# Attention and MLP kernel: the second head's query projection cut into tiles, placed beside the first head's steps, into a bank of the PV accumulators

## The chip, the cores and the metric

One core of a Trainium2 chip. The metric is the device time of one execution in microseconds (us), as a median of several. The kernel before takes 1239.27 us (3 runs, 1239.21 to 1239.27).

## The reference, cut to what matters

```python
xn = layernorm(x)                                   # x: 2048 x 512
q = (xn @ wq).reshape(1, 2048, 32, 128)             # 32 heads of 128
p = softmax(einsum("bhqd,bhkd->bhqk", q, k_cache) * 128 ** -0.5)
o = einsum("bhqk,bhkd->bhqd", p, v_cache)           # 2048 keys
s = o.reshape(1, 2048, 4096) @ wo
h = relu(xn @ w1 + b1) ** 2                         # 1792 hidden
return x + s * silu(h @ w2 + b2)
```

All inputs are bfloat16. The queries are worked off in four blocks of 512, and in each block the 32 heads one after the other: 128 "heads" g in all, of eight steps each.

## The kernel before: what the change touches

TensorE runs, per step, a scores group (`gen_scores`), a group of products with V (`gen_pv`), and between them up to three matmuls of fill-in work (`fill_one`): query projections of later heads, MLP, output products. ScalarE (ACT) does the exponentials; VectorE (DVE) the casts out of PSUM. PSUM has eight banks: four for scores (psA), two for PV (psO), two for fill-in work (psF).

The opening differs. For head 0 the layernorm is not ready, so its four query tiles of 128 are normalised, transposed and projected one by one, and a step handles one query tile against half of the keys. So PV of steps 0 to 3 (query tiles 0 and 1) writes psO bank 0, and only steps 4 to 7 write bank 1.

```python
def first_proj(i):                     # head 0, query tile i: four matmuls of 128 columns
    for c in range(NDC):
        t_proj[0] = E(PE, partial(_mm, out=bankF(0)[:, i * P:(i + 1) * P],
                                  lhsT=wq_sb[:, 0, c, :], rhs=xnT[:, c, i * P:(i + 1) * P], ...),
                      deps=[t_wqfill[0], tok_xT[0][i], t_q0[i - 1] if i else None], ...)

def first_evac(i):                     # its cast to bfloat16, which the scores wait for
    t_evac[0] = t_q0[i] = E(DV, partial(_copy, out=qt_sb[:, 0, i * P:(i + 1) * P], ...))

def job_proj(g):                       # heads 1 to 127: four matmuls of 512 columns, one per fill_one
    def mm(n, bank):
        t = E(PE, partial(_mm, out=bankF(bank), lhsT=wq_sb[:, i, n, :], rhs=xnT[:, n, js], ...), ...)
    def evac(bank, step):
        t_evac[g] = E(DV, partial(_copy, out=qt_sb[:, g % NQS, :], in_=bankF(bank)), ...)

# order of the loads on the SyncE queue          # the opening, from the first scores on
load_v0(0)                                       gen_scores(0); gen_scores(1)
load_v0(1)                                       first_proj(1); first_evac(1)
fill_wq(1)                                       gen_pv(0); gen_scores(2); first_transpose(2)
fill_k(1)                                        gen_scores(3); first_proj(2); first_evac(2)
                                                 gen_pv(1); gen_scores(4); first_transpose(3)
                                                 gen_scores(5); gen_pv(2); first_proj(3); first_evac(3)
                                                 fill_one(0); fill_one(0)     # half of job_proj(1)
                                                 gen_pv(3); gen_scores(6); gen_scores(7)
                                                 fill_one(0); fill_one(0)     # the other half
                                                 gen_pv(4); gen_pv(5)         # then the main loop
```

The softmax here doesn't subtract the row's maximum and nothing guards it: scores larger than these inputs give would overflow.

## Time and profile before

| | before |
|---|---|
| time, median | 1239.27 us |
| span in the profile | 1237.5 us |
| TensorE's share of the chain that ended last | 98% |
| first scores start | 7.63 us |
| head 3's projection starts | 21.97 us |
| between the two ("the stage") | 14.34 us |

Everything that the change moves on TensorE lies between the first scores and the first matmul of head 3's projection. VectorE's timeline of the kernel before (start, duration, what it did, idle time ahead of it) shows the casts that TensorE waits for:

```profile
14.20 0.29 DVE L179 CAST qt_sb<-psF 128x128 bf16<-128x128 f32 x1 [0.70 <-PE psF L152]
16.41 0.69 DVE L179 CAST qt_sb<-psF 128x512 bf16<-128x512 f32 x1 [1.92 <-PE psF L152]
17.02 0.42 DVE L179 COPY o_un<-psO 128x258 f32<-128x258 f32 x1
...
20.53 0.69 DVE L165 TENSOR_TENSOR o_bf<-o_un,rden 128x512 bf16<-128x512 f32 x1
21.14 0.68 DVE L179 CAST qt_sb<-psF 128x512 bf16<-128x512 f32 x1
21.75 0.16 DVE L179 CAST b1f<-psF 128x14 f32<-128x14 bf16 x1
```

The first is head 0's query tile 3, the second head 1's queries, the fifth head 2's queries; the last three stand one behind the other, and the hole that they make in TensorE's timeline is the last of the opening:

```profile
20.98 0.59 PE L152 MATMUL psA<-qt_sb,kT 128*128 128x512 bf16 x2
21.97 0.38 PE L152 MATMUL psF<-xnT,wq_sb 128*128 128x512 bf16 x1 [0.40 <-DVE b1f L179]
```

Two matmuls of 512 columns end their occupancy at 20.98 + 0.43 = 21.41, so 0.56 us are empty. The view names b1f, which ended last; by the code the matmul waits for its psF bank, which the cast of head 2's queries frees. The packed trace, read one instruction at a time, agrees: the semaphore instruction of TensorE that ends this wait starts at 21.87, 0.04 behind the end of that cast (21.83) and ahead of the end of b1's (21.91).

### The profile page before, as it was taken

To read this page: it belongs to the slowest core of one execution; us is meant where nothing else is said; L and a number is where in the kernel's file an instruction comes from. 1 tells how busy PE (TensorE), PEld (TensorE's weight loads), DVE (VectorE), ACT (ScalarE), POOL (GpSimd) and SP (SyncE) were. 2 spreads that over 40 slices of the span, in tenths; PEclk is the share of its full clock that TensorE was granted. 3 is DMA by queue.
4 is the path that set the end of the run, shared out by engine and by line. 5 is a ranking of instruction groups with operands and counts; after the bars stand their busy time and mean duration, and the time that the engine had idled before them with its cause. 6 is when DMAs were issued, how large, how long until landed. Compare 5 with 4: busy or idle time off the path is not lost.

```text
span 1237.5 us, 26703 instructions
## 1 busy us (share of the span) xinstructions
PE 1221.4 (99%) x11666; PEld 818.6 (66%) x11873; DVE 472.9 (38%) x953; ACT 1053.6 (85%) x1044; POOL 32.0 (3%) x73
## 2 busy tenths in 40 slices
PE   9999999999999999999999999999999999999998
PEld 7666666666666666666666666666666666666666
DVE  4453333244435332334444532233344333324333
ACT  7888888888888888888888888888888888888885
POOL 1010000000002000000000200000000000000000
PEclk9999999999999999999999999999999999999999
DMA  9999988777888787877788888787788788778761
GB/s 209 217 235 180 191 178 140 128 139 140 144 154 166 143 161 133 133 141 146 135 132 169 171 141 142 137 150 137 133 145 149 147 154 157 138 134 146 146 123 31
DMA packets 686868, 185.41 MB, mean 150 GB/s; under 512 B 673536, under 2 KB 685568, under 8 KB 686752
## 3 DMA queue, kind: packets, MB, share of 16 engines
q1 hardware_dynamic: 684656, 179.62, 80.7%
q0 software_dynamic: 1424, 3.81, 1.1%
q8 instruction: 94, 1.54, 0.5%
q10 hardware_dynamic: 672, 0.26, 0.1%
q14 instruction: 22, 0.18, 0.1%
HBM read 96.60 MB, written 2.10 MB: 80 GB/s over the span
## 4 chain that ended last, share of the span: by engine, by line
PE 98%; issue 1%; DVE 1%; DMA 0%; ACT 0%; POOL 0%; DVEq 0%
PE psO L157 38%; PE psA L152 35%; PE psF L152 25%; PE psA L157 0%; DMA x_ln<-in_A_x_dram 0%; DVE out_t L165 0%; PE psF L196 0%; DVE tmp_t L175 0%; ACT pT L161 0%; DVE xnT L179 0%; DVE st_t L200 0%; DVE o_bf L165 0%; DVE qt_sb L179 0%; POOL rstd L165 0%; DVE o_un L179 0%
## 5 line engine op out<-in xcount | busy, mean ns | idle before, releaser
L161 ACT ACTIVATE pT<-psA 128x1024 bf16<-128x1024 f32 x1024 | 1043.6, 1023 | 165.0 <-PE psA L152 119.7
L157 PEld LDWEIGHTS psO<-v_sb,pT 128*128 128x128 bf16 x8192 | 547.9, 98 | 240.8 <-issue 13.1
L157 PE MATMUL psO<-v_sb,pT 128*128 128x129 bf16 x8192 | 631.2, 220 | 0.9 <-ACT pT L161 0.4
L152 PE MATMUL psA<-qt_sb,kT 128*128 128x512 bf16 x1837 | 562.3, 379 | 10.2
L179 DVE COPY o_un<-psO 128x258 f32<-128x258 f32 x256 | 97.4, 422 | 398.5 <-PE psO L157 397.7
L152 PE MATMUL psF<-xnT,wq_sb 128*128 128x512 bf16 (+1 forms) x514 | 167.1, 374 | 0.8 <-DVE b1f L179 0.4
L152 PE MATMUL psF<-wo_all,oT 128*128 128x512 bf16 x479 | 163.4, 379 | 0.1
L152 PEld LDWEIGHTS psA<-qt_sb,kT 128*128 128x128 bf16 x2032 | 156.9, 98 | 0.1
L179 DVE CAST qt_sb<-psF 128x512 bf16<-128x512 f32 (+1 forms) x131 | 88.7, 677 | 103.7 <-PE psF L152 98.0
L152 PEld LDWEIGHTS psF<-xnT,wq_sb 128*128 128x128 bf16 x524 | 50.6, 98 | 60.8 <-issue 1.2
L165 DVE TENSOR_TENSOR o_bf<-o_un,rden 128x512 bf16<-128x512 f32 x128 | 88.5, 692 | 4.7 <-DVE rden L183 0.3
L171 DVE TENSOR_SCALAR r_t<-psF,b1f 128x512 bf16<-128x512 f32 x56 | 42.0, 750 | 116.9 <-PE psF L152 116.9
L152 PEld LDWEIGHTS psF<-wo_all,oT 128*128 128x128 bf16 x480 | 46.9, 98 | 56.4
L152 PE MATMUL psF<-xnT,w_sb 128*128 128x512 bf16 x224 | 77.1, 379 | 0.0
L152 PE MATMUL psF<-w_sb,h2T 128*128 128x512 bf16 x223 | 73.7, 379 | 0.0
L152 PEld LDWEIGHTS psF<-w_sb,h2T 128*128 128x128 bf16 x224 | 21.9, 98 | 26.4
L152 PEld LDWEIGHTS psF<-xnT,w_sb 128*128 128x128 bf16 x224 | 21.9, 98 | 26.4
L165 DVE TENSOR_TENSOR z_t<-psF,b2bc 128x512 f32<-128x512 f32 x16 | 11.1, 692 | 68.3 <-PE psF L152 63.8
L165 DVE TENSOR_TENSOR acc<-psF,acc 128x512 f32<-128x512 f32 x28 | 19.3, 689 | 30.0 <-PE psF L152 30.0
L208 POOL DMA_DIRECT2D out_dram<-out_t x12 | 6.7, 554 | 890.4 <-DVE out_t L165 890.4
L183 DVE RECIPROCAL rden<-o_un 128x4 f32<-128x4 f32 x128 | 22.9, 179 | 4.4
L165 DVE TENSOR_TENSOR h2T<-r_t 128x512 bf16<-128x512 bf16 x56 | 23.8, 425 | 1.9
(44 smaller groups left out, 162.2 us busy)
## 6 DMA issues: line engine op xcount, KB each, us to landing
v_sb<-in_A_v_cache_dram SPq DMA_DIRECT2D x127, 512.0 KB, 4.7
wq_sb<-in_A_wq_dram SPq DMA_DIRECT2D x127, 128.0 KB, 3.4
wo_all<-in_A_wo_dram SPq DMA_DIRECT2D x4, 1024.0 KB, 6.3
w_sb<-in_B_w_dram SPq DMA_DIRECT2D x14, 256.0 KB, 5.1
oT<-o_bf SPq DMA_TRANSPOSE x128, 4.0
x_t<-in_A_x_dram POOLq DMA_DIRECT2D x16, 128.0 KB, 3.2
kT<-in_A_k_cache_dram SPq DMA_TRANSPOSE x127, 4.5
x_ln<-in_A_x_dram SPq DMA_DIRECT2D x15, 128.0 KB, 3.7
```

The costliest lines, as they stand in the source:

```text
L152: return e.matmul(out, lhsT, rhs, start=start, stop=stop)
L157: return e.matmul(out, lhsT, rhs, start=start, stop=stop, skip_group_check=True)
L161: return e.activation(out, in_, func, bias=bias, scale=scale)
L165: return e.tensor_tensor(out, in0, in1, op)
L171: return e.tensor_scalar(out, in0, scalar1=scalar1, scalar2=scalar2, op0=op0, op1=op1)
L179: return e.tensor_copy(out, in_)
L183: return e.reciprocal(out, in_)
L208: return e.dma_start(out, in_)
```

## The change

Head 1's projection leaves its two places near the end of the opening. It is done per query tile, right behind head 0's projection of the same tile (tile 0 together with tile 1), where TensorE is meant to be waiting for ACT or VectorE anyway. The psF banks are taken then, so it writes psO bank 1, which nobody needs between the transposes of the first keys and step 4; one cast empties it. Its weights must come earlier, so their load moves ahead of the two value loads.

```diff
+    def second_proj(i):
+        for c in range(NDC):
+            t_proj[1] = E(PE, partial(_mm, out=bankO(1)[:, i * P:(i + 1) * P],
+                                      lhsT=wq_sb[:, 1, c, :], rhs=xnT[:, c, i * P:(i + 1) * P],
+                                      start=(c == 0), stop=(c == NDC - 1)),
+                          deps=[t_wqfill[1], tok_xT[0][i], t_k0[1]], inc=(c == NDC - 1))
+
+    def second_evac():
+        t_evac[1] = E(DV, partial(_copy, out=qt_sb[:, 1, :], in_=bankO(1)), deps=[t_proj[1]])
 ...                                                      (gen_pv)
                   deps=[t_exp[pi], t_v0[k % 2] if g == 0 else t_vfill[g], t_ones,
+                        t_evac[1] if g == 0 and b == 1 else None,
 ...                                                      (list of fill-in jobs)
-    for g in range(1, NG):
+    for g in range(2, NG):
 ...                                                      (loads)
+    fill_wq(1)
     load_v0(0)
     load_v0(1)
-    fill_wq(1)
 ...                                                      (opening)
     first_evac(1)
+    second_proj(0)
+    second_proj(1)
     gen_pv(0)
 ...
     first_evac(2)
+    second_proj(2)
     gen_pv(1)
 ...
     first_evac(3)
+    second_proj(3)
+    second_evac()
-    fill_one(0)
-    fill_one(0)
     gen_pv(3)
     gen_scores(6)
     gen_scores(7)
-    fill_one(0)
-    fill_one(0)
     gen_pv(4)
```

## The prediction

> **What bounds the kernel now.** I first read the busy shares and the chain that ended last on the page of the kernel before.
>
> ```profile
> PE 1221.4 (99%) x11666; PEld 818.6 (66%) x11873; DVE 472.9 (38%) x953; ACT 1053.6 (85%) x1044; POOL 32.0 (3%) x73
> ...
> PE 98%; issue 1%; DVE 1%; DMA 0%; ACT 0%; POOL 0%; DVEq 0%
> PE psO L157 38%; PE psA L152 35%; PE psF L152 25%; PE psA L157 0%; DMA x_ln<-in_A_x_dram 0%; DVE out_t L165 0%; PE psF L196 0%; DVE tmp_t L175 0%; ACT pT L161 0%; DVE xnT L179 0%; DVE st_t L200 0%; DVE o_bf L165 0%; DVE qt_sb L179 0%; POOL rstd L165 0%; DVE o_un L179 0%
> ```
>
> TensorE (PE) carries 98% of the chain: PV products (psO), scores (psA), and projections, MLP and output products (psF). Busy time alone would not prove it, since matmul ends are modelled, but the chain says the same. So the change can gain in two ways only: fewer array cycles, or fewer holes between matmuls.
>
> Then I listed TensorE's whole-run waits by releaser. After the 1.0 us at the start there are three: 0.4 us for ACT pT, 0.4 us for DVE b1f, 0.2 us for DVE xnT. That view hides short holes, because a matmul counts as busy until its modelled end. So I read the opening in TensorE's timeline (start, duration, count, what it waited for):
>
> ```profile
> 7.63 1.05 PE L157 MATMUL psA<-qt_sb,kT 128*128 128x128 bf16 x16
> 8.52 0.39 PE L152 MATMUL psF<-xnT,wq_sb 128*128 128x128 bf16 x4
> 9.35 0.63 PE L157 MATMUL psO<-v_sb,pT 128*128 128x129 bf16 x8 [0.45 <-ACT pT L161]
> ...
> 11.16 0.40 PE L152 MATMUL psF<-xnT,wq_sb 128*128 128x128 bf16 x4
> 11.40 0.62 PE L157 MATMUL psO<-v_sb,pT 128*128 128x129 bf16 x8
> 12.04 0.61 PE L157 MATMUL psA<-qt_sb,kT 128*128 128x128 bf16 x8
> 12.64 0.40 PE L196 MATMUL psF<-ident,xn_t 128*128 128x128 bf16 x4
> ...
> 13.77 0.82 PE L152 MATMUL psF<-xnT,wq_sb 128*128 128x128 bf16 x5
> 14.43 0.62 PE L157 MATMUL psO<-v_sb,pT 128*128 128x129 bf16 x8
> 14.88 1.06 PE L157 MATMUL psA<-qt_sb,kT 128*128 128x128 bf16 x16
> 15.77 0.59 PE L152 MATMUL psF<-xnT,wq_sb 128*128 128x512 bf16 x2
> 16.21 1.07 PE L157 MATMUL psO<-v_sb,pT 128*128 128x129 bf16 x16
> 17.24 0.59 PE L152 MATMUL psA<-qt_sb,kT 128*128 128x512 bf16 x2
> ```
>
> The reader takes starts from it, not durations. Sixteen scores start at 7.63 and the next group at 8.52, so a 128-column matmul occupies 0.89/16 = 0.056 us; a pair of 512-column ones takes 16.21 - 15.77 = 0.44, or 0.216 each. A hole is the next start less the start plus count times that. Two things to see: a hole of 9.35 - (8.52 + 0.225) = 0.60 us before the first PV group, which waits for the first exponential (ACT, 8.27 to 9.29), and the second head's four 512-column projections sitting where no hole is (two inside the x5 row at 13.77, which lacks one record, and two at 15.77). Smaller holes: 11.85 to 12.04 (0.19, for the cast of the first head's third query tile, DVE 11.60 to 11.89), 12.49 to 12.64 (0.15, for xn_t), and 17.11 to 17.24 (0.13, for the cast of the second head's queries, DVE 16.41 to 17.10). After 22 us the timeline shows a closed row of groups.
>
> **What the Trainium skill says.** "TensorE: Matmul & The Clock Gate", section "Back-to-back issue gap", gives the warm spacing as N/2.4 + 2.5 ns: 56 ns at 128 columns, 216 at 512. The trace agrees (0.056 and 0.216 us). The same section's "sustained" 81 and 131 ns are not what this trace shows, so I use the measured ones. "PSUM — Partial Sum Buffer", section "PSUM bank collisions raise a hardware error", asks for guards by bank, not by address: so PV of query tiles 2 and 3 of head 0, which write the borrowed bank, must wait for the whole cast out of it, which is the wait the change adds. "DMA: Bandwidth & Descriptors", section "Queues, rings and completion order", says that descriptors on each DMA engine's ring are consumed in order. So moving the weight load ahead of the two value loads brings it forward and pushes them back. The trace agrees in tendency: first-half values, second-half values and weights, issued at 3.06, 3.5 and 4.16, landed after 4.9, 5.5 and 5.2 us, that is at 7.96, 9.05 and 9.36.
>
> **The change part by part.**
>
> *Removed:* the second head's projection, 4 x 0.216 = 0.86 us of TensorE, all on the path: 0.43 before PV step 3 and 0.43 before PV step 4.
>
> *Added:* 16 matmuls of 128 columns, 16 x 0.056 = 0.90 us; the array work is thus equal within 0.04 us. Their places decide the gain.
> - Tiles 0 and 1 (8 x 0.056 = 0.45) go after the first head's second projection, at 8.75, into the hole of 0.60. They end at about 9.20, before the PV group is released at 9.35. Cost 0.
> - Tile 2 (0.225) goes before PV step 1: 11.39 to 11.61. That PV ends at 12.06 instead of 11.85, and the scores behind it could not start before 12.04 anyway. Cost about 0.02, and the 0.15 hole for xn_t swallows it. Cost 0.
> - Tile 3 (0.225) goes in after the fourth projection, at 13.995, where there is no hole. Cost 0.225.
>
> *Sum up to PV step 4:* 0.225 - 0.86 = -0.64 us.
>
> *Moved:* the 512-column cast of the second head's queries (0.69 us on DVE) leaves 16.41 for about 14.5, after the cast of tile 3 (14.20 to 14.49). It ends near 15.2. PV step 4, the first user of the borrowed bank, would start at 15.57: the new wait is met with about 0.4 us to spare. The scores of head 1 no longer wait for that cast: another -0.13, the hole at 17.11.
>
> *Do the dependences follow the shift?* Working forward: PV step 3 runs 14.22 to 14.67; the scores of step 6 need the tile-3 cast, which releases at 14.49 + 0.15 = 14.64 (0.15 is the cast-to-start delay seen at 11.89 to 12.04), so they just fit. Their exponential starts 0.65 later, as before (15.53 - 14.88), at 15.32 and ends near 16.34. Scores of steps 6 and 7 and PV steps 4 and 5 end at 14.67 + 0.89 + 0.91 = 16.47, where the first scores of head 1 reuse the buffer freed at 16.34 to 16.40. They fit by under 0.1 us. So those scores start at about 16.47 instead of 17.24: -0.77 us.
>
> *Transfers.* The weights of head 1, now first of three, should land between 7 and 8 (estimate from the landings above: two thirds of a microsecond after the last x tile at 2.55 + 4.2 = 6.7), and are needed at 8.75. First-half values should land near 9.36 - 1.09 = 8.3, since all three still end at 9.36 and the second half takes 9.05 - 7.96 = 1.09; needed at 9.35. Second-half values land near 9.4, needed at about 11.6. None bites. Everything queued behind keeps its place and amount.
>
> *After 22 us* the comparison of the two instruction orders shows no other difference on any engine: the projection came out of slots of the opening, not of the fill-in rhythm of the main loop. Only the parity of the two psF banks flips, and both banks are alike. So the end moves by the same 0.77: 1239.27 - 0.77 = 1238.5 us, or 0.06%.
>
> **The rivals.**
> 1. *The gain is lost to a wait in the opening.* The hole of 0.56 us at 21.41 to 21.97 (the next projection waits for the cast of head 2's queries, DVE 21.14 to 21.82, behind the reciprocal and the normalisation of head 0) stays and could grow if its DVE chain did not move. For: DVE is in order there. Against: that chain begins when PV step 7 ends, which moves with TensorE. If it stood still, about nothing would be gained: 1239.2.
> 2. *The early weights come late and TensorE waits in order.* For: the load's issue took 2.28 us in its old place, so that queue is congested. Against: it goes in ahead of what congested it. If it landed as late as before (9.36), the tiles would run 9.4 to 9.85, PV 0 and what follows would move by 0.5, and the gain would shrink to about 0.3: 1239.0. The same if the first-half values were over 1 us later than before.
> 3. *ACT takes over in the opening.* It idles 0.91 us before the exponential of step 6; TensorE arriving earlier uses that up, and at 16.47 the margin is under 0.1 us. If exponentials bound there, some 0.1 to 0.3 of the 0.77 is lost: 1238.7.
> 4. *More than counted.* If the 0.56 hole closed as well, the gain would be 1.3: 1237.9. I see no part of the change that closes it.
>
> **Range and chances.** Every path but one lies in 1237.9 to 1239.2, and the three runs before lay within 0.06 us. A chip other than that one may differ by some tenths; so 1238.0 to 1239.1 for 8 in 10. Two per cent is 24.8 us, thirty times the gain, and everything the change touches lies in the first 22 us: within 2% has 0.99, the rest is for a surprise.
>
> **What would show it right or wrong.** In the changed kernel's timeline: eight psO<-xnT,wq_sb matmuls at about 8.75 and the first PV still at 9.35 (later would mean weights or values late); scores of step 4 still near 12.05; PV step 3 near 14.2; the cast of the second head from psO ending near 15.2, and no hole of TensorE before PV step 4; the first 512-column scores near 16.5; the hole near 21 still about 0.5 us long and 0.8 earlier. A shift of the opening that does not reappear at the end would make the argument wrong, as it would show that something other than TensorE's order sets the end.

## The result, and the profile after

1238.70 us (6 runs, 1238.42 to 1238.91) against 1239.28 (6 runs, 1239.21 to 1239.48) for the kernel before. The ratio is 0.9995, with a 95% interval of 0.9982 to 1.0008: "same" at 2%. A ratio here is the mean time of one kernel's fast runs over that of the other's of the same rounds, so not quite the ratio of the medians quoted. The interval is wider than the effect, but no run of one kernel overlaps the other's, here or in the repeat below. What rests on tenths of a microsecond below rests on the traces, and the times only agree with it.

TensorE's timeline of the changed kernel:

```profile
7.76 1.05 PE L157 MATMUL psA<-qt_sb,kT 128*128 128x128 bf16 x16 [0.23 <-DVE qt_sb L179]
8.65 0.39 PE L152 MATMUL psF<-xnT,wq_sb 128*128 128x128 bf16 x4
8.87 0.61 PE L152 MATMUL psO<-xnT,wq_sb 128*128 128x128 bf16 x8
9.48 0.63 PE L157 MATMUL psO<-v_sb,pT 128*128 128x129 bf16 x8
...
11.53 0.39 PE L152 MATMUL psO<-xnT,wq_sb 128*128 128x128 bf16 x4
11.76 0.62 PE L157 MATMUL psO<-v_sb,pT 128*128 128x129 bf16 x8
12.21 0.61 PE L157 MATMUL psA<-qt_sb,kT 128*128 128x128 bf16 x8
12.78 0.40 PE L196 MATMUL psF<-ident,xn_t 128*128 128x128 bf16 x4
...
14.13 0.39 PE L152 MATMUL psO<-xnT,wq_sb 128*128 128x128 bf16 x4
14.36 0.62 PE L157 MATMUL psO<-v_sb,pT 128*128 128x129 bf16 x8
14.81 1.06 PE L157 MATMUL psA<-qt_sb,kT 128*128 128x128 bf16 x16
15.70 1.07 PE L157 MATMUL psO<-v_sb,pT 128*128 128x129 bf16 x16
16.61 0.59 PE L152 MATMUL psA<-qt_sb,kT 128*128 128x512 bf16 x2
...
21.34 0.38 PE L152 MATMUL psF<-xnT,wq_sb 128*128 128x512 bf16 x1 [0.40 <-DVE b1f L179]
```

Read it from the first scores. Before, the first PV group came 9.35 - 7.63 = 1.72 us behind them; now 9.48 - 7.76 = 1.72, with eight more matmuls in between. The scores of step 6 (the second x16 row) come at 7.05 instead of 7.25, PV step 4 at 7.94 instead of 8.58, head 1's first scores at 8.85 instead of 9.61. The stage takes 21.34 - 7.76 = 13.58 us instead of 14.34: 0.76 less.

The new cast is where it was meant to be, in VectorE's timeline of the changed kernel:

```profile
14.33 0.29 DVE L179 CAST qt_sb<-psF 128x128 bf16<-128x128 f32 x1 [0.70 <-PE psF L152]
14.56 0.69 DVE L179 CAST qt_sb<-psO 128x512 bf16<-128x512 f32 x1
```

It ends at 15.25, ahead of PV step 4 at 15.70. The shift lasts to the end: head 1's first scores start 17.24 - 16.61 = 0.63 us earlier by the clock of the span, and VectorE's last instruction starts at 1234.61 instead of 1235.24, again 0.63.

The profile shows 0.63 and not 0.76 because in this one profile the first scores came 0.13 later. The matmuls of the opening have two durations. In the profile of the changed kernel those that transpose the first keys (of psO<-ident,kT) are at 314 ns in the median and 219 at the least; in that of the kernel before the median is 219 and the most is 314:

```profile
L196 PE MATMUL psO<-ident,kT x16: 219/314/314, 4.8 to 6.6; 128*128 128x128 bf16 x16
```

```profile
L196 PE MATMUL psO<-ident,kT x16: 219/219/314, 4.8 to 6.4; 128*128 128x128 bf16 x16
```

The two views give the count, the least, the median and the greatest duration. The ends of matmuls are modelled, but the starts in the packed traces say the same: the step from one start to the next falls from 107 to 56 ns 4.5 us after the first matmul in the kernel before, and 5.3 us after it in the changed one. So TensorE was still at its slow pace for longer. The Trainium skill, "TensorE: Matmul & The Clock Gate", section "Part 1: The HAM clock gate (the "warmup" mystery)", says that the clock is released by a free-running window, at a moment that varies by half a microsecond either way. The window may be the cause, but the half microsecond is not what is seen here: over the eleven profiles the step falls anywhere from 2.9 us (x7) to 5.7 us (x6) after the first matmul. Most of that does not reach the first scores, which started from 7.51 to 7.97. The mean granted clock reads 1.00 in all eleven and shows none of it, because the clock records begin only where the step falls (within 0.1 us, in the ten profiles that have records). In two of the eleven (x7 and x8 below) a late landing of the first keys held the first scores up instead. Either way it is chance from run to run, and the repeat of the same changed kernel below shows it.

### The profile page after: what moved, and what is told of

The parts are those of the page before. It is cut to its first block, busy times and chain, and to the rows that moved or that the text cites. A ratio compares the mean times of both kernels' runs of the same rounds, so it can differ in the third digit from the quotient of the medians.

```text
span 1236.8 us, 26934 instructions
## 1 busy us (share of the span) xinstructions
PE 1232.1 (100%) x11885; PEld 819.5 (66%) x11885; DVE 472.5 (38%) x953; ACT 1054.5 (85%) x1044; POOL 32.1 (3%) x73
## 4 chain that ended last, share of the span: by engine, by line
PE 99%; DVE 0%; issue 0%; POOL 0%; DVEq 0%; POOLq 0%
PE psO L157 38%; PE psA L152 36%; PE psF L152 25%; PE psA L157 0%; DVE out_t L165 0%; PE psO L196 0%; DVE tmp_t L175 0%; PE psF L196 0%; DVE qt_sb L179 0%; PE psO L152 0%; DVE o_bf L165 0%; DVE o_un L179 0%; DVE xnT L179 0%; POOL warm L187 0%; DVE rden L183 0%
## 5 line engine op out<-in xcount | busy, mean ns | idle before, releaser
L152 PE MATMUL psA<-qt_sb,kT 128*128 128x512 bf16 x2032 | 604.3, 379 | 0.0
```

Of the source, the lines that this page charges most:

```text
L152: return e.matmul(out, lhsT, rhs, start=start, stop=stop)
```

## The experiments

Nine runs in three series, each timed in five rounds; all are "same" at 2%, so the stage decides, read from one profile of each run, and the times only agree. "Mean difference" is the mean time less that of the kernel before in the same series.

| run | median, us | before, us | mean difference | first scores | stage, us |
|---|---|---|---|---|---|
| before | | 1239.28 | | 7.63 | 14.34 |
| the change | 1238.70 | 1239.28 | -0.62 | 7.76 | 13.58 |
| x0_after_again | 1238.51 | 1239.27 | -0.77 | 7.56 | 13.58 |
| x1_order_only | 1239.25 | 1239.27 | +0.09 | 7.57 | 14.35 |
| x2_old_order | 1239.21 | 1239.27 | -0.03 | 7.67 | 14.22 |
| x3_miss_hole | 1238.97 | 1239.27 | -0.33 | 7.57 | 14.03 |
| x5_no_tiles012 | 1238.47 | 1239.21 | -0.71 | 7.51 | 13.59 |
| x6_late_cast | 1238.87 | 1239.21 | -0.45 | 7.97 | 13.79 |
| x4_b1_early | 1238.02 | 1239.21 | -1.26 | 7.64 | 13.02 |
| x7_no_tiles | 1238.48 | 1239.42 | -0.91 | 7.79 | 13.54 |
| x8_whole_late | 1239.30 | 1239.42 | -0.12 | 7.78 | 14.22 |

All gave the reference's result within its tolerance, even the two that are wrong (x5 and x7): one head of 32 with wrong queries in a quarter of the rows does not show there. For those two the comparison says nothing. It also means that the comparison would not notice an error in what the change moves, head 1's first queries; that these are right rests on the code.

The theory: the sixteen small matmuls gain only because they stand where TensorE waited; the loads are hidden. The rivals: the new order of loads, the borrowed bank with its early cast, or merely taking the projection off steps 3 and 4, wherever it goes.

**x0_after_again: the control.** No edit.

> The changed kernel once more, as the control of this series and to see how far its opening varies between profiles. My theory: TensorE's holes of the opening alone make the difference, so about 0.6 us under the kernel before (0.4 to 0.8), near 1238.7. In its profile the first scores start at 7.76 again if the 0.13 us by which the opening came later in the profile of the changed kernel is a lasting effect of the new order of loads; at about 7.63 if it was chance from run to run. Rival (the gain is noise of the chip): no difference from the kernel before beyond 0.2 us.

Measured: -0.77 on average, first scores at 7.56, stage 13.58 to the hundredth. So the 0.13 was chance, and the stage repeats.

**x1_order_only: the loads alone.**

```diff
 # kernel before
+    fill_wq(1)
     load_v0(0)
     load_v0(1)
-    fill_wq(1)
```

> The kernel before with one thing changed: the weights of head 1 are loaded ahead of the two value loads. Theory: loads are hidden, so the time is that of the kernel before within 0.1 us, near 1239.3, and the first PV group stays at about 9.35. Rival A (the new order itself delays the opening): 1239.4, first scores at about 7.76. Rival B (the gain of the change comes from the order of the loads): 1238.7.

Measured: a stage of 14.35 against 14.34, and medians 0.02 apart. Both rivals fall: the order neither gains nor costs by itself.

**x2_old_order: the change without the new order of loads.**

```diff
 # changed kernel
-    fill_wq(1)
     load_v0(0)
     load_v0(1)
+    fill_wq(1)
```

> The changed kernel with the weights of head 1 again behind the two value loads. They then land at about 9.36, while the first two tiles of the second head's projection stand in TensorE's order at 8.75 to 8.9. Theory: TensorE waits there, the tiles run from about 9.4 to 9.85, the first PV group starts near 9.9 instead of 9.48, and about 0.4 of the gain goes: 1239.1 (1239.0 to 1239.2). Rival (the load's place does not matter): 1238.7, first PV group at about 9.45.

Measured: the stage takes 14.22, so 0.64 of the 0.76 are lost. TensorE's timeline of this run names the cause:

```profile
8.56 0.39 PE L152 MATMUL psF<-xnT,wq_sb 128*128 128x128 bf16 x4
9.59 0.62 PE L152 MATMUL psO<-xnT,wq_sb 128*128 128x128 bf16 x8 [0.64 <-DMA wq_sb<-in_A_wq_dram]
10.04 0.62 PE L157 MATMUL psO<-v_sb,pT 128*128 128x129 bf16 x8
```

The weights were issued at 4.16 and landed after 5.4 us, at 9.56, and everything behind them in TensorE's order waited. I had expected 0.4; they landed 0.2 later than in the profile of before, which I had taken the landing from. The median, 1239.21, is 0.01 over my range. The moved load gains nothing but is a condition for nearly all of the gain. This is the prediction's rival 2, made to happen; it leaves 0.12 us of the stage's gain, where the prediction said about 0.3.

**x3_miss_hole: tiles 0 and 1 behind the first PV group.**

```diff
 # changed kernel
-    second_proj(0)
-    second_proj(1)
     gen_pv(0)
+    second_proj(0)
+    second_proj(1)
```

> The changed kernel with tiles 0 and 1 of the second head's projection placed behind the first PV group instead of ahead of it: the same sixteen matmuls, but these eight no longer fall into the wait for the first exponential. Theory: the hole of about 0.6 us is back and the eight cost their full 0.45 us: 1239.15 (1239.0 to 1239.3), PV step 3 near 14.8 instead of 14.36. Rival (what gains is the taking of the projection off the steps 3 and 4, wherever it goes): 1238.7.

Measured: a stage of 14.03, 0.45 longer, which is the eight matmuls' full 8 x 0.056. The median, 1238.97, is 0.03 under the range I gave (its five runs lie from 1238.90 to 1239.12). The hole is back:

```profile
9.29 0.63 PE L157 MATMUL psO<-v_sb,pT 128*128 128x129 bf16 x8 [0.45 <-ACT pT L161]
9.76 0.61 PE L152 MATMUL psO<-xnT,wq_sb 128*128 128x128 bf16 x8
```

One group further on, the same work goes from free to fully paid.

**x5_no_tiles012: tiles 0 to 2 taken out** (wrong).

```diff
 # changed kernel
-    second_proj(0)
-    second_proj(1)
 ...
-    second_proj(2)
```

> The changed kernel without tiles 0, 1 and 2 of the second head's projection (twelve matmuls of 128 columns, 0.67 us of array time); the cast then reads leftovers in three quarters of the bank, so the result is wrong on purpose. Theory: these twelve lie in holes and cost nothing, so the time stays that of the changed kernel within 0.15 us, near 1238.7, and PV step 3 starts near 14.3 as in it. Rival (array work counts wherever it stands): 0.67 us less, 1238.0.

Measured: 13.59 (21.10 - 7.51) with twelve matmuls fewer, against 13.58. They cost nothing measurable. The median, 1238.47, is 0.08 under the range I gave but 0.04 from the repeat of the changed kernel. TensorE's timeline of this run has the two ends of the stage:

```profile
7.51 1.05 PE L157 MATMUL psA<-qt_sb,kT 128*128 128x128 bf16 x16
...
21.10 0.38 PE L152 MATMUL psF<-xnT,wq_sb 128*128 128x512 bf16 x1 [0.40 <-DVE b1f L179]
```

**x7_no_tiles: tile 3 taken out as well** (wrong; the cast waits for what it reads instead).

```diff
 # x5_no_tiles012
-    second_proj(3)
 ...
-        ... in_=bankO(1)), deps=[t_proj[1]])
+        ... in_=bankO(1)), deps=[t_k0[1], t_proj[0]])
```

> The changed kernel without any tile of the second head's projection (all sixteen matmuls gone, 0.90 us of array time); the cast reads leftovers, so the result is wrong on purpose. It is the floor of what any placing of this projection can reach. Read from the first scores to the first matmul of head 3's projection (14.34 us in the kernel before, 13.58 in the changed one). Theory: only tile 3 stood on the path, with 0.225, but the scores of step 6 then wait for the cast of the first head's tile 3, so 0.14 to 0.2 are saved: 13.40 (13.35 to 13.46), time about 0.15 under the changed kernel. Rival (the array work counts where it stands): 0.9 less, 12.7.

Measured: 13.54, only 0.04 under the changed kernel. I was wrong by 0.14: tile 3 is nearly free too. Without it TensorE reaches the scores of step 6 at about 14.6 and waits for the cast of head 0's tile 3, which ends at 14.36 + 0.29 = 14.65; the scores start at 14.80, 7.01 behind the first scores against 7.05 with tile 3. In timelines of VectorE and TensorE of this run:

```profile
14.36 0.29 DVE L179 CAST qt_sb<-psF 128x128 bf16<-128x128 f32 x1 [0.70 <-PE psF L152]
```

```profile
14.80 1.05 PE L157 MATMUL psA<-qt_sb,kT 128*128 128x128 bf16 x16
```

So the whole second projection now costs 0.04 us on the path.

**x8_whole_late: the borrowed bank without the tiles.**

```diff
 # changed kernel; second_proj(0), (1) and (2) taken out
-    second_proj(3)
+    for c in range(NDC):
+        t_proj[1] = E(PE, partial(_mm, out=bankO(1), lhsT=wq_sb[:, 1, c, :], rhs=xnT[:, c, 0:QB],
+                                  start=(c == 0), stop=(c == NDC - 1)), ...)
```

> The changed kernel with the second head's projection in one piece, four matmuls of 512 columns into the borrowed bank, at the place of tile 3: bank, cast and order of loads as in the changed kernel, but nothing in the holes. Theory: 0.864 us stand on the path instead of 0.225, so the stage from the first scores to head 3's projection takes 13.58 + 0.64 = 14.22 us (14.15 to 14.28) and the time is about 1239.15. Rival (the borrowed bank and the early cast bring the gain, the splitting into tiles is not needed): 13.6 and 1238.6.

Measured: 14.22, as expected; the median is 0.15 over what I wrote, as is that of the kernel before in this series over 1239.27. Bank and loads are those of the change, the cast is as early as the whole projection allows, and 0.64 of the 0.76 are gone. In TensorE's timeline of this run the four stand undivided in front of PV step 3:

```profile
14.15 1.03 PE L152 MATMUL psO<-xnT,wq_sb 128*128 128x512 bf16 x4
15.01 0.62 PE L157 MATMUL psO<-v_sb,pT 128*128 128x129 bf16 x8
```

The rival falls for all but the 0.12 that is left: PV step 4 comes 16.36 - 7.78 = 8.58 behind the first scores, as in the kernel before, and head 1's first scores 9.49 instead of 9.61. That is the hole of 0.13 for the old cast, closed by the earlier cast alone. The other 0.64 need the tiles, and the bank makes the tiles possible.

**x6_late_cast: how much slack has the new wait?**

```diff
     def second_evac():
+        E(DV, partial(_copy, out=qt_sb[:, 2, :], in_=bankO(1)), deps=[t_proj[1]])
         t_evac[1] = E(DV, ...)
```

> The changed kernel with the cast out of the borrowed bank doubled: one more copy of the same 512 columns ahead of it, about 0.60 us of DVE, so that the wait of PV step 4 for the bank ends later. Theory: the cast ended at 15.25 and PV step 4 started at 15.70, with 0.15 from a cast's end to a start on TensorE, so 0.3 us of the 0.60 are slack and the other 0.3 go onto the path: PV step 4 near 16.0 and 1239.0 (1238.9 to 1239.1). Rival A (the wait is far from binding): 1238.7. Rival B (the wait binds already): the whole 0.6, 1239.3.

Measured: the stage grew by 0.21 to 13.79, so 0.60 - 0.21 = 0.39 us were slack and not 0.3; the prediction's own "about 0.4 us to spare" was nearer. The median, 1238.87, is 0.03 under my range. VectorE's and TensorE's timelines of this run:

```profile
14.77 1.29 DVE L179 CAST qt_sb<-psO 128x512 bf16<-128x512 f32 x2
```

```profile
16.11 1.08 PE L157 MATMUL psO<-v_sb,pT 128*128 128x129 bf16 x16
```

The pair of casts ended at 16.05 (16.06 by the rounded view) and PV step 4 started at 16.11: 0.05 from a cast's end to the start, where x7 shows 0.15 for the scores behind their cast. The packed traces, read one instruction at a time, show where these two differ. In x6 the weight load ahead of the first matmul carries the wait itself and starts at 16.11. In x7 a separate semaphore instruction (0.05 us) carries it; it starts at 14.69, 0.04 behind the cast's end, then comes the weight load at 14.77, with a second semaphore to wait for, and the matmul at 14.80. Neither rival holds: the wait does not bind, but has under half a microsecond left.

**x4_b1_early: the hole that stays.** The small transpose of b1 goes behind PV step 5; its slot in the main loop is left empty, so that all else keeps its place.

```diff
 # changed kernel
-    jobs = [(3, 3, job_b1(), None)]
+    jobs = [(3, 3, (1, lambda n, bank: None, None), None)]
 ...                              (an empty job frees no bank and changes none)
     gen_pv(5)
+    _, b1_mm, b1_evac = job_b1()
+    b1_mm(0, 0)
+    t_bankF[0] = b1_evac(0, 0)
```

> The changed kernel with the small transpose of the bias b1 done behind PV step 5 instead of between the projections of head 2 and head 3; its slot in the main loop is left empty, so the rhythm of the fill-in work stays. The projection of head 3 then takes the other psF bank, which has long been free, instead of waiting for the cast of head 2's queries. Theory: the hole of 0.57 us (20.77 to 21.34 in the changed kernel) closes and no other opens: 1238.1 (1238.0 to 1238.3), 0.5 under the changed kernel. Rival (the wait only moves: ACT or the next cast takes its place): 1238.6 or more, with a hole of TensorE within the 5 us behind it.

Measured: stage 13.02, 0.56 less, and 1238.02 us, as the theory said. In TensorE's timeline of this run head 3's projection (the third row) follows without a hole, 20.23 + 0.43 = 20.66:

```profile
19.78 0.62 PE L157 MATMUL psO<-v_sb,pT 128*128 128x129 bf16 x8
20.23 0.59 PE L152 MATMUL psA<-qt_sb,kT 128*128 128x512 bf16 x2
20.66 0.38 PE L152 MATMUL psF<-xnT,wq_sb 128*128 128x512 bf16 x1
20.88 0.62 PE L157 MATMUL psO<-v_sb,pT 128*128 128x129 bf16 x8
```

No wait took its place in the groups up to 40 us. The b1 transpose is worked off in one matmul but had held a psF bank, which put two projections into the same bank with only one slot between. This version is faster than both kernels: 1.26 us under the kernel before on average, 0.10%, and the slowest of its five runs (1238.17) is under the fastest run of either.

## Why the prediction was right

The time (1238.7 against 1238.5) lies in the range. The mechanism was right, one pair of terms was not. By its steps:

- *Tiles 0 and 1 in the hole, cost 0:* right. 1.72 us to the first PV group in both kernels; x3 and x5 confirm it from both sides.
- *Tile 2, cost 0.02, then swallowed:* right. The scores of step 4 come at 12.21 - 7.76 = 4.45 instead of 4.41, the transposes behind them at 5.02 instead of 5.01.
- *Tile 3, "where there is no hole. Cost 0.225":* mis-sized. x7 shows 0.04. The view of the kernel before had no hole there because half of the old projection filled it; with that half gone, a wait for the cast of head 0's tile 3 appears. So the first 0.43 that the sum removes was in part a filler as well (without any projection the scores of step 6 come 7.25 - 7.01 = 0.24 earlier, not 0.43), and both terms were too large by 0.19. Their difference, the only thing the time shows, was right, because the same overlooked wait stands in both terms and cancels: 0.20 measured, 0.43 - 0.225 = 0.21 predicted. The prediction had both numbers at hand (14.64 for the release, 14.67 for the arrival) and called it "just fit" instead of asking what would be there without tile 3.
- *The second 0.43 and the 0.13 for the old cast:* right. PV step 4 comes 0.64 earlier, head 1's first scores 0.76 (predicted 0.64 and 0.77).
- *Transfers:* right. The weights landed at 3.06 + 4.2 = 7.3, the values at 3.54 + 4.9 = 8.4 and near 9.5; predicted 7 to 8, 8.3 and 9.4. x2 shows what the old order would have done.
- *Rivals:* ACT did not bind, the hole of 0.56 us stayed as said (0.57, from 20.77 to 21.34), and the shift reached the end undiminished.
- *What was left out:* the start of the opening varies by chance with the moment at which TensorE reaches its full pace. It took 0.13 us of the profiled run's gain, and the six runs spread over 0.49 us. The repeat gave 0.77; that the same kernel gave 0.62 in the first series shows how far the times alone can be trusted.

## What to carry to other kernels

Before moving work, list the holes of the limiting engine by starts and counts, not by its busy share, and ask which work could run in each and what must have landed by then; here eight matmuls cost nothing ahead of one group and 0.45 us behind it. A place without a hole may be one only because what stands there fills it, so cost a move from what the engine would wait for with that work taken out. And ask of a small job which buffer it takes in a rotation: one matmul of 14 columns cost 0.56 us by putting two projections into the same bank.

## What the Trainium skill lacked or had wrong

- "TensorE: Matmul & The Clock Gate", section "Back-to-back issue gap": its isolated gap (56 and 216 ns at 128 and 512 columns) is what the streams run at, with a weight load ahead of every matmul; its "sustained" 81 and 131 ns were not seen (0.056 and 0.216 us).
- The same page, Part 1: it lets the moment of release vary by half a microsecond either way; here the step between starts falls from 107 to 56 ns at 2.9 to 5.7 us after the first matmul, over eleven profiles. It tells of the free-running window, but not that the mean granted clock of a profile can read 1.00 while the matmuls of the first 4 to 7 us run at the slow pace: the records of these profiles begin only where the pace changes.
- No page that I read gives the delay from a VectorE cast's end to the TensorE start that waits for it. The runs show 0.04 to 0.05 us to the TensorE instruction that carries the wait. The matmul starts 0.15 us behind the cast's end where that is a separate semaphore instruction ahead of the weight load (x7, scores), and 0.05 us where it is the weight load itself (x6, a PV group).
